# Earlier decoding of packed MLP weights, and earlier loads and splits for the first expert page, in a fused attention, MLP and mixture-of-experts kernel

## The chip, the cores and the metric

The kernel runs on one core of one Trainium2 chip. The metric is device time in microseconds (us) from the program's start to its end: the median of three runs. The five engines of the core that appear below are TensorE (PE; its weight loads are PEld), VectorE (DVE), ScalarE (ACT), GpSimd (POOL) and SyncE (SP), which here only starts transfers. Each engine works through its own list of instructions strictly in order, and waits for the others by semaphores.

## What is computed

```python
def reference(**kwargs):
    # attention: 4 batches, 8 heads, 768 positions, 64 wide;
    # a position sees 4 sink positions and a window of 128
    scores = np.where(is_sink | in_window, scale * q @ k.T, -1e9)
    a = softmax(scores)
    x = (a @ v).transpose(0, 2, 1, 3).reshape(3072, 512)
    # MLP, 512 -> 2048 -> 512
    h = x @ w_in
    x = (h - np.tanh(h)) @ w_out
    # top-1 mixture of 8 experts, 512 -> 1024 -> 512
    e_idx = np.argmax(x @ w_gate + modality_bias[modality_id], axis=1)
    for e in range(8):
        mask = e_idx == e
        out[mask] = gate_w[mask, None] * (np.maximum(x[mask] @ w1[e], 0) @ w2[e])
    return out
```

Everything is float32. The MLP weights arrive in memory as 64-bit words.

## The kernel before

**Precision.** A float32 matrix product is made of three faster products: each operand is split into a high part (a rounding cast, mostly on ScalarE, line 209) and a low part (a subtraction, on GpSimd or VectorE, line 214), and high by high, high by low and low by high are summed.

**The three stages.** The 3072 tokens are handled in 12 chunks of 256. A chunk needs 8 attention units (96 in all; a unit U has scores `s`, line 315 for the first 14 units, a masked row maximum `e`, line 324 on VectorE, an exponential, a normalisation with `sm`, lines 329 to 338, a transposition `T`, lines 348 and 349, and a product with the values `R`, lines 406 to 410). A chunk's MLP then runs over 16 slices f of the hidden width: `L1` (line 176) makes `h` from the chunk's tokens `xt` and the slice `wi`, `gact` (lines 187 to 192) makes `g` from two slices, and `L2` (line 246) adds to `acc` with the slice `wo`. The last stage is the experts: tokens are sorted into pages of 256 rows of one expert each, 13 pages being run always; the page's weights are loaded (`m_wload`, line 745, tile `mr`) and split (`m_wsplit`, ScalarE's cast at line 753, tile `mh`, and VectorE's subtraction at line 754, tile `ml`). The page's list of tokens is loaded by `m_list` (line 762, tile `mpl`) and turned into indices on VectorE (lines 764 and 766, tiles `mi` and `ms`). The order of the first three pages is known after chunk 10 has been routed.

**Decoding.** All 32 half-slices of the MLP weights (`wi0` to `wi15`, `wo0` to `wo15`) are loaded once (`w_load`, line 135, tile `raw`, 512 KB each, issued by SyncE) and decoded once (`w_decode`) out of the 64-bit words, during the first 160 us. A decode is three VectorE instructions (lines 145, 147 and 149), one ScalarE cast and one GpSimd subtraction.

**What sets the order.** Each step is emitted with a due time, and the steps are sorted by it; a scheduler that builds the program then sets the final order within each engine. Sixteen units of due time are one chunk, so one attention unit takes two. The due times come from a table, `self.o`, in line 45: `wl` and `wls` are the first due time and the spacing of the weight loads, `wd` and `wds` those of the decodes, `mwl` and `mws` how far ahead of its use a page's weight slice is loaded and split. `m_events` never lets a step of the first pages be due before the routing is known (`max(t + d, t0)`).

Of the kernel before, what the change touches and what calls it, by code (L numbers as in the profile page):

```python
# [40 lines left out]
class Kern:  # L41
    def __init__(self, tc, a):
        self.tc, self.nc, self.a = tc, tc.nc, a
        self.Wi, self.Wo = {}, {}
        self.o = dict(tc='a', xa='g', mt0=-0.28, gz='v', mxe=11, lx='v', nf=14, efh='a', trc=-14.17, tpf=-1.86, xhi='v', vhi='a', vlo='g', qhi='a', khi='v', sT='a', tr='a', ev='a', glo='g', whi='a', wlo='g', gk=0, wl=-8.54, wls=1.25, wd=-3.86, wds=1.05, wo=1, bs=2, be=3, bE=3, bV=1, bg=2, btr=1, bxt=1, pt={'h': 'h', 's': 'r', 'T': 'r', 'R': 'R', 'x': 'R', 'y': 'R'}, pb=(('r', 2), ('h', 2), ('R', 2)), tl=-9.97, ts=-5.86, tv=-4.34, tsv=-2.34, tS=-5.24, dS=0.07, tN=-4, dN=0.5, tT=-1.78, dT=0.35, tPV=-0.39, txs=-0.28, tg=0.64, tre=0.05, trl=0.48, trr=3.39, u0=-15.64, g=2, lag=3.4, raw=2, sp=2, ghi='a', qlo='g', klo='v', eh='v', xlo='v', x2=4, me=13, mxl=8.77, mxt=1.5, mlag=1.45, mwl=9.99, mws=3.27, mm=0, ev0='v', ghi0='a', vhi0='a', sT0='a', qhi0='a', xlo0='g', eh0='v', y=2)

    def e(self, k, start):
        return self.o.get(k + "0", self.o[k]) if start else self.o[k]
# [786 lines left out]
    def m_events(self, add, g, t, t0=-1e9, ts=(0, 1)):  # L835
        n8 = FF // P
        o = self.o
        at = lambda d, fn, *a: add(max(t + d, t0), fn, *a)
        at(-o["me"], self.m_expert, g)
        x0 = o["mxe"] if g == 1 else o["mxl"]  # L840
        if g < EARLY and t0 > 0:
            add(t0, self.m_list, g)
        else:
            at(-x0 - .01, self.m_list, g)
        at(-x0, self.m_xload, g, ts)
        for j in ts:
            at(-o["mxt"] + 0.5 * j, self.m_xT, g, j, ts)
            at(n8 + o["mlag"] - 0.5, self.m_out, g, j)
        for f in range(n8):
            at(f - o["mwl"], self.m_wload, g, f)  # L850
            at(f - o["mws"], self.m_wsplit, g, f)
            at(f, self.m_L1, g, f, ts)
            at(f + o["mlag"], self.m_L2, g, f, ts)

# [205 lines left out]
```

## Time and profile before

| | us |
|---|---|
| three runs | 1157.36, 1158.56, 1164.47 |
| median | 1158.56 |
| profiled execution | 1158.06 |
| its span, first to last instruction | 1156.3 |
| TensorE busy in the span | 1109.8 |
| VectorE busy in the span | 845.4 |

The three runs show the time of whole executions. The profile is of one execution; the 1.76 us between its time and its span lie around the first and the last instruction. Busy times are of the whole span and are averages over stages that differ: the first 160 us (attention and decoding), the steady chunks, and the pages from about 835 us on.

### The profile page before, as it was taken

How to read it: one execution, taken by the hardware profiler on the slowest of the kernel's cores; microseconds unless marked ns; L12 is line 12 of the kernel's file. 1: busy time of each engine (PE TensorE's matmuls, PEld its weight loads, DVE VectorE, ACT ScalarE, POOL GpSimd, SP SyncE). 2: the span in 40 equal slices, each digit the busy share in tenths (PEclk: the TensorE clock that was granted, in tenths of full speed). 3: DMA queues.
4: the chain of work that ended last, by engine and by line, in shares of the span. 5: the costliest groups of instructions: out<-in, count | busy, mean ns of one | idle time of the engine just before them, and what ended most of it. 6: DMA issues, size and time to landing. Idle time of an engine off the chain costs nothing. (4 is left out here: it accounts for less than half of the span.)

```text
span 1156.3 us, 22180 instructions
## 1 busy us (share of the span) xinstructions
PE 1109.8 (96%) x7143; PEld 978.2 (85%) x7143; DVE 845.4 (73%) x2244; ACT 696.1 (60%) x1669; POOL 586.4 (51%) x847
## 2 busy tenths in 40 slices
PE   7999889999999999999999999999899999999995
PEld 3467678998999999998999998998788989999984
DVE  3389988787888878798888789765687566666640
ACT  3566656666667666667576666664746555555531
POOL 2257775667676767676676767662203211121111
PEclk9999999999999999999999999999999999999998
DMA  6356422223232322222131322100857776677600
GB/s 201 92 188 220 142 71 49 81 74 69 75 70 70 70 78 62 88 65 86 52 94 52 92 65 68 60 10 19 304 188 247 239 231 219 214 233 239 211 21 22
DMA packets 74957, 136.79 MB, mean 118 GB/s; under 512 B 16144, under 2 KB 51216, under 8 KB 74832
## 3 DMA queue, kind: packets, MB, share of 16 engines
q1 hardware_dynamic: 70064, 122.40, 35.0%
q0 software_dynamic: 4768, 12.87, 3.4%
q8 instruction: 59, 0.97, 0.4%
q14 instruction: 66, 0.54, 0.2%
HBM read 122.60 MB, written 12.91 MB: 117 GB/s over the span
## 5 line engine op out<-in xcount | busy, mean ns | idle before, releaser
L176 PE MATMUL h<-xt,wi 128*128 128x256 f32 x2304 | 349.7, 290 | 10.7 <-ACT wi L209 4.3
L176 PEld LDWEIGHTS h<-xt,wi 128*128 128x128 f32 x2304 | 313.5, 193 | 31.1 <-ACT wi L209 6.1
L246 PE MATMUL acc<-wo,g 128*128 128x512 f32 x1152 | 313.9, 399 | 6.0 <-ACT g L209 5.1
L246 PEld LDWEIGHTS acc<-wo,g 128*128 128x128 f32 x1152 | 201.9, 189 | 39.0 <-ACT g L209 5.7
L754 DVE TENSOR_TENSOR ml<-mr,mh 128x1024 fp32r<-128x1024 f32 x104 | 129.3, 1247 | 57.9 <-ACT mh L753 56.7
L214 POOL TENSOR_TENSOR g<-gy,g 128x512 fp32r<-128x512 f32 x96 | 130.9, 1364 | 74.0 <-ACT g L209 70.1
L803 PE MATMUL mh<-mxt,mh 128*128 128x256 f32 (+1 forms) x832 | 154.4, 282 | 1.0 <-ACT mxt L791 0.7
L803 PEld LDWEIGHTS mh<-mxt,mh 128*128 128x128 f32 x832 | 135.7, 191 | 9.5 <-ACT mxt L791 0.9
L820 PE MATMUL macc<-mh,mg 128*128 128x512 f32 x400 | 141.6, 399 | 0.2
L753 ACT CAST mh<-mr 128x1024 fp32r<-128x1024 f32 x104 | 108.9, 1051 | 44.5 <-PE macc L820 29.6
L356 POOL TENSOR_SCALAR_AFFINE_SELECT X<-fl 128x512 fp32r<-128x512 f32 (+1 forms) x192 | 113.2, 612 | 41.8 <-DVE fl L386 23.5
L829 POOL DMA_INDIRECT out_dram<-mo,mi x25 | 26.2, 1046 | 205.7 <-ACT mo L828 202.0
L326 ACT ACTIVATE e<-e,nm 128x160 f32<-128x160 f32 x192 | 81.7, 426 | 79.9 <-DVE nm L324 71.2
L803 PE MATMUL mh<-mxt,ml 128*128 128x256 f32 (+1 forms) x416 | 117.0, 282 | 0.0
L191 ACT ACTIVATE u<-u,kt 128x512 f32<-128x512 f32 x96 | 69.4, 723 | 45.8 <-DVE h L190 30.8
L324 DVE CUSTOM_DVE_ANT_0 e<-s,mask 128x160 f32<-128x160 f32 x192 | 61.3, 319 | 37.0 <-PE T L349 28.4
L214 DVE TENSOR_TENSOR K<-k,K 64x448 fp32r<-64x448 f32 x82 | 85.3, 1040 | 2.7
L214 POOL TENSOR_TENSOR B<-q,A 128x256 fp32r<-128x256 f32 x82 | 70.6, 861 | 31.5 <-ACT A L209 31.2
L820 PEld LDWEIGHTS macc<-mh,mg 128*128 128x128 f32 x400 | 74.4, 189 | 13.3 <-DVE mg L807 1.0
L806 ACT ACTIVATE mg<-mh 128x256 fp32r<-128x256 f32 (+1 forms) x104 | 39.2, 377 | 75.1 <-PE mh L803 70.6
L187 ACT ACTIVATE u<-h 128x512 f32<-128x512 f32 x96 | 56.4, 588 | 40.0 <-PE h L176 39.7
L803 PEld LDWEIGHTS mh<-mxt,ml 128*128 128x128 f32 x416 | 79.3, 191 | 0.0
(230 smaller groups left out, 2196.1 us busy)
## 6 DMA issues: line engine op xcount, KB each, us to landing
mr<-in_moe_w_dram SPq DMA_DIRECT2D x104, 512.0 KB, 4.7
k<-in_k_dram SPq DMA_DIRECT2D x82, 224.0 KB, 2.6
v<-in_v_dram SPq DMA_DIRECT2D x96, 128.0 KB, 2.4
q<-in_q_dram SPq DMA_DIRECT2D x82, 128.0 KB, 2.3
rawi<-in_moe_w_in_dram SPq DMA_DIRECT2D x16, 512.0 KB, 6.2
rawo<-in_moe_w_out_dram SPq DMA_DIRECT2D x16, 512.0 KB, 5.4
x2d<-x SPq DMA_DIRECT2D x24, 256.0 KB, 2.1
k<-in_k_dram SPq DMA_DIRECT2D x14, 112.0 KB, 2.6
```

Of the source, the lines that this page charges most:

```text
L176: nc.tensor.matmul(h, w[:, wl, k * P:(k + 1) * P], x[:, xl, k], start=(n == 0), stop=(n == 11))
L187: nc.scalar.activation(u, h, AF.Square)
L191: nc.scalar.activation(u, u, AF.Relu, bias=self.kt, accum_out=self.over[:, n:n + 1])
L214: (self.nc.vector if eng == "v" else self.nc.gpsimd).tensor_tensor(out=out, in0=a, in1=b, op=ALU.subtract)
L246: nc.tensor.matmul(o, g[:, gl, q:q + P], w[:, wl], start=(f == 0 and n == 0), stop=(f == NF - 1 and n == 2))
L324: nc.vector.tensor_tensor_reduce(out=e, in0=s[:, P:QW], in1=self.mask[min(i, 2)], scale=-0.125, scalar=3.0e38, op0=ALU.add, op1=ALU.min, a ...
L326: nc.scalar.activation(e, e, AF.Exp, bias=nm, scale=-1.0, accum_out=u["sm"][:, t:t + 1])
L356: self.nc.gpsimd.affine_select(out=out, in_=in_, pattern=[[0, n], [s, P]], base=0, channel_multiplier=-s, compare_op=ALU.is_gt if prev els ...
L753: nc.scalar.copy(hi, r)
L754: nc.vector.tensor_sub(lo, r, f32(hi))
L803: nc.tensor.matmul(h, wt[:, k * P:(k + 1) * P], x[:, xl, k, c0:c0 + w], start=(n == 0), stop=(n == 11))
L820: nc.tensor.matmul(self.macc[g][t], gt[:, gl, i * P:(i + 1) * P], w[:, DM:], start=(f == 0 and n == 0), stop=(f == n8 - 1 and n == 2))
```

## The change

Four due times of the MLP weights change, and the first page gets its own two lead times. The loads and decodes begin earlier, and are spaced wider, so that one pair (`wi` and `wo` of one f) falls to about one attention unit; the loads move by nearly the same distance as the decodes. The first page's weights are due 14 f ahead of their use in place of 9.99 to load, and 7 f in place of 3.27 to split.

```diff
-        self.o = dict(... wl=-8.54, wls=1.25, wd=-3.86, wds=1.05, ...
-                      mwl=9.99, mws=3.27, ...)
+        self.o = dict(... wl=-21.0, wls=1.9, wd=-14.0, wds=1.8, ...
+                      mwl=9.99, mwl0=14.0, mws0=7.0, mws=3.27, ...)
...
         for f in range(n8):
-            at(f - o["mwl"], self.m_wload, g, f)
-            at(f - o["mws"], self.m_wsplit, g, f)
+            at(f - (o["mwl0"] if g == 0 else o["mwl"]), self.m_wload, g, f)
+            at(f - (o["mws0"] if g == 0 else o["mws"]), self.m_wsplit, g, f)
```

In the built program the first difference shows on VectorE between the row maxima of the units 4 and 5 (`e4_1` and `e5_1`; `nm` is the maximum, `s` the scores, `ypi` and `ypo` scratch of a decode, `yo` its result). Before:

```order
L317 COPY_PREDICATED s4_1_389<-mgt_74,s4_1_389 128x128
L324 ISA e4_1_393,nm4_1_392<-s4_1_389,mask1_118 128x160
L324 ISA nm4_1_392 128x1
L330 RECIPROCAL sm4_384<-sm4_384 128x2
L324 ISA e5_0_428,nm5_0_427<-s5_0_424,mask0_107 128x160
L324 ISA nm5_0_427 128x1
L317 COPY_PREDICATED s5_1_431<-mgt_74,s5_1_431 128x128
L324 ISA e5_1_435,nm5_1_434<-s5_1_431,mask1_118 128x160
L324 ISA nm5_1_434 128x1
L211 CAST xt0_736<-xp0_1_399 128x256
```

After, from `e5_0` to `e5_1`:

```order
L324 ISA e5_0_482,nm5_0_481<-s5_0_478,mask0_107 128x160
L324 ISA nm5_0_481 128x1
L145 TENSOR_SCALAR ypo2_522<-rawo2_276 128x512
L330 RECIPROCAL sm4_418<-sm4_418 128x2
L317 COPY_PREDICATED s5_1_485<-mgt_74,s5_1_485 128x128
L147 SCALAR_TENSOR_TENSOR ypo2_522<-rawo2_276,ypo2_522 128x512
L149 SCALAR_TENSOR_TENSOR yo2_521<-rawo2_276,ypo2_522 128x512
L145 TENSOR_SCALAR ypi3_558<-rawi3_294 128x512
L147 SCALAR_TENSOR_TENSOR ypi3_558<-rawi3_294,ypi3_558 128x512
L211 CAST xt0_826<-xp0_1_443 128x256
L324 ISA e5_1_489,nm5_1_488<-s5_1_485,mask1_118 128x160
L324 ISA nm5_1_488 128x1
```

Between `e5_0` and `e5_1` stand one whole decode, two instructions of the next, and a cast of the MLP's input; before, only a selection of scores stood there. By the last row maximum of unit 9, 15 of the 32 decodes are through VectorE in place of 3, by the end of chunk 0's first `gact` 17 in place of 5, and by unit 16 31 in place of 27.

TensorE's list around unit 4's scores (`s4`) and unit 2's values product (`R2`). Before:

```order
L315 MATMUL s4_0_382<-k4_234,q4_233 128x288
L315 MATMUL s4_1_389<-k4_234,q4_233 128x288
L406 MATMUL R2_398<-sTn2_376,v2_272 64x256
L407 MATMUL R2_398<-X2_379,v2_272 64x128
L410 MATMUL R2_398<-X2_379,v2_272 64x256
L348 MATMUL T3_411<-ident_69,e3_0_296 128x128
L349 MATMUL T3_411<-ident_69,e3_0_296 128x128
L348 MATMUL T3_411<-ident_69,e3_1_303 128x128
```

After:

```order
L315 MATMUL s4_0_416<-k4_242,q4_241 128x288
L315 MATMUL s4_1_423<-k4_242,q4_241 128x288
L406 MATMUL R2_442<-sTn2_402,v2_284 64x256
L407 MATMUL R2_442<-X2_405,v2_284 64x128
L176 MATMUL h0_0_844<-xt0_826,wi0_383 128x256
L410 MATMUL R2_442<-X2_405,v2_284 64x256
L176 MATMUL h0_0_844<-xt0_826,wi0_383 128x256 x2
L348 MATMUL T3_457<-ident_69,e3_0_310 128x128
L349 MATMUL T3_457<-ident_69,e3_0_310 128x128
L348 MATMUL T3_457<-ident_69,e3_1_317 128x128
```

The first three MLP products stand inside unit 2's values product; ahead of unit 10's first scores (`s10_0`) stand 18 MLP products in place of 9.

At the first page, SyncE's list of transfers, from the first weight slice `mr0_0` on (`mpl1` and `mpl2` are the token lists of the next two pages). Before:

```order
L745 DMA mr0_0_11532<-in_moe2_w_dram 128x1024
L759 TENSOR_LOAD order_344
L759 ISA x2
L762 ISA
L762 DMA mpl1_11543<-xs_63 128x2x2
L759 TENSOR_LOAD order_344
L759 ISA x2
L762 ISA
L762 DMA mpl2_11558<-xs_63 128x2x2
L745 ISA
```

After:

```order
L745 ISA
L745 DMA mr0_1_11534<-in_moe2_w_dram 128x1024
L745 ISA
L745 DMA mr0_2_11536<-in_moe2_w_dram 128x1024
L745 ISA
L745 DMA mr0_3_11538<-in_moe2_w_dram 128x1024
L745 ISA
L745 DMA mr0_4_11540<-in_moe2_w_dram 128x1024
L759 TENSOR_LOAD order_360
L759 ISA x2
L762 ISA
L762 DMA mpl1_11551<-xs_63 128x2x2
```

The slices 1 to 4 now follow the slice 0 directly, and the token lists come behind them.

VectorE's list at the same place, behind the activation step of slices 8 and 9 of chunk 11. Before:

```order
L192 SCALAR_TENSOR_TENSOR gy11_4_11646<-gy11_4_11646,h11_8_11606 128x512
L764 CAST mi0_11528<-mpl0_11526 128x2
L766 SCALAR_TENSOR_TENSOR ms0_11530<-mpl0_11526 128x2
L764 CAST mi1_11545<-mpl1_11543 128x2
L766 SCALAR_TENSOR_TENSOR ms1_11547<-mpl1_11543 128x2
L764 CAST mi2_11560<-mpl2_11558 128x2
L766 SCALAR_TENSOR_TENSOR ms2_11562<-mpl2_11558 128x2
L190 TENSOR_TENSOR h11_10_11657<-u11_5_11705,h11_10_11657 128x512
L192 SCALAR_TENSOR_TENSOR gy11_5_11706<-gy11_5_11706,h11_10_11657 128x512
L754 TENSOR_TENSOR ml0_0_11737<-mr0_0_11532,mh0_0_11736 128x1024
```

After:

```order
L192 SCALAR_TENSOR_TENSOR gy11_4_11658<-gy11_4_11658,h11_8_11614 128x512
L764 CAST mi0_11528<-mpl0_11526 128x2
L766 SCALAR_TENSOR_TENSOR ms0_11530<-mpl0_11526 128x2
L190 TENSOR_TENSOR h11_10_11671<-u11_5_11721,h11_10_11671 128x512
L192 SCALAR_TENSOR_TENSOR gy11_5_11722<-gy11_5_11722,h11_10_11671 128x512
L754 TENSOR_TENSOR ml0_0_11634<-mr0_0_11532,mh0_0_11633 128x1024
L754 TENSOR_TENSOR ml0_1_11668<-mr0_1_11534,mh0_1_11667 128x1024
L754 TENSOR_TENSOR ml0_2_11691<-mr0_2_11536,mh0_2_11690 128x1024
L190 TENSOR_TENSOR h11_12_11735<-u11_6_11780,h11_12_11735 128x512
L764 CAST mi1_11553<-mpl1_11551 128x2
L766 SCALAR_TENSOR_TENSOR ms1_11555<-mpl1_11551 128x2
L764 CAST mi2_11568<-mpl2_11566 128x2
```

The index steps of the pages 1 and 2 (`mi1`, `ms1`, `mi2`, `ms2`) no longer stand ahead of `h11_10`, but behind `h11_12`.

## Rows read from the trace of the kernel before

**Rows 1.** The page: busy time of each engine.
```profile
PE 1109.8 (96%) x7143; PEld 978.2 (85%) x7143; DVE 845.4 (73%) x2244; ACT 696.1 (60%) x1669; POOL 586.4 (51%) x847
```

**Rows 2.** Busy time by stretch: start and end, length, then each engine, clock, DMA.
```profile
core 0: us, PE busy (x) PEld busy (x) DVE busy (x) ACT busy (x) POOL busy (x), PEclk, DMA share, GB/s
24.23:62.75 38.52, 38.03 (x93) 18.34 (x94) 14.17 (x53) 17.50 (x58) 11.04 (x24) 1.00 0.43 130
62.75:152.22 89.47, 77.36 (x401) 58.81 (x401) 86.14 (x185) 59.33 (x150) 67.34 (x81) 0.96 0.53 176
220.00:280.00 60.00, 59.20 (x410) 54.27 (x409) 49.14 (x147) 40.29 (x109) 42.24 (x64) 1.00 0.28 72
```

**Rows 3.** Timeline of TensorE: start, time, engine, line, operation, count, idle before.
```profile
5.66 4.80 PE L315 MATMUL s<-k,q 64*128 64x288 f32 x8 [5.66 <-DMA k<-in_k_dram]
...
24.23 2.39 PE L315 MATMUL s<-k,q 64*128 64x288 f32 x4
47.67 0.42 PE L348 MATMUL T<-ident,e 128*128 128x128 f32 x1
...
62.75 2.28 PE L315 MATMUL s<-k,q 64*128 64x288 f32 x4
64.96 3.57 PE L176 MATMUL h<-xt,wi 128*128 128x256 f32 x15
71.08 1.45 PE L176 MATMUL h<-xt,wi 128*128 128x256 f32 x10 [0.56 <-POOL wi L214]
76.69 0.27 PE L349 MATMUL T<-ident,e 128*128 128x128 f32 x1
...
152.22 0.38 PE L176 MATMUL h<-xt,wi 128*128 128x256 f32 x1 [1.42 <-DVE xt L211]
```

**Rows 4.** VectorE by kind, from 24.23 to 62.75 us.
```profile
L324 DVE CUSTOM_DVE_ANT_0 e<-s,mask 128x160 f32<-128x160 f32 x12 | 3.9, 324 | 15.0 <-PE T L349 14.2 <-PE s L315 0.8
```

**Rows 5.** VectorE's timeline in a run of decodes.
```profile
88.01 0.68 DVE L149 SCALAR_TENSOR_TENSOR yo<-rawo,ypo 128x512 int32<-128x512 int32 x1
88.61 0.69 DVE L147 SCALAR_TENSOR_TENSOR ypi<-rawi,ypi 128x512 int32<-128x512 int32 x1
```

**Rows 6.** VectorE and GpSimd by kind, from 62.75 to 152.22 us.
```profile
L149 DVE SCALAR_TENSOR_TENSOR yo<-rawo,ypo 128x512 int32<-128x512 int32 x15 | 10.2, 680 | 0.1
L214 POOL TENSOR_TENSOR wo<-yo,wo 128x512 fp32r<-128x512 f32 x14 | 18.6, 1328 | 6.0 <-ACT wo L209 6.0
```

**Rows 7.** TensorE's waits from 62.75 to 152.22 us: total, times, longest.
```profile
PE h L176 <- ACT wi L209: 4.3, 6, 1.3
PE h L176 <- POOL wi L214: 2.4, 4, 0.9
```

**Rows 8.** Timeline at the first page: SyncE, VectorE, ScalarE, TensorE.
```profile
813.89 1.77 SPq L762 DMA_DIRECT2D mpl<-xs  x2
815.91 18.20 SPq L745 DMA_DIRECT2D mr<-in_moe_w_dram  x16
...
817.61 0.17 DVE L764 CAST mi<-mpl 128x2 int32<-128x2 f32 x1 [4.05 <-DMA mpl<-xs]
...
819.43 0.72 ACT L191 ACTIVATE u<-u,kt 128x512 f32<-128x512 f32 x1 [3.55 <-DVE h L190]
826.02 1.05 ACT L753 CAST mh<-mr 128x1024 fp32r<-128x1024 f32 x1 [1.12 <-DMA mr<-in_moe_w_dram]
830.18 0.61 ACT L209 CAST g<-gy 128x512 fp32r<-128x512 f32 x1
...
817.89 2.00 PE L246 MATMUL acc<-wo,g 128*128 128x512 f32 x8
830.85 1.40 PE L246 MATMUL acc<-wo,g 128*128 128x512 f32 x4 [3.93 <-ACT g L209]
832.73 3.18 PE L246 MATMUL acc<-wo,g 128*128 128x512 f32 x8 [0.48 <-POOL g L214]
```

**Rows 9.** Busy time by stretch, TensorE waiting for the first page.
```profile
820.00:840.00 20.00, 15.35 (x86) 12.80 (x85) 16.97 (x18) 17.48 (x27) 4.98 (x4) 0.91 1.02 406
```

More of the change, by code (lines that the diff above doesn't have):

```diff
@@ L44, in __init__ @@
         self.Wi, self.Wo = {}, {}
-        self.o = dict(tc='a', xa='g', mt0=-0.28, gz='v', mxe=11, lx='v', nf=14, efh='a', trc=-14.17, tpf=-1.86, xhi='v', vhi='a', vlo='g', qhi='a', khi='v', sT='a', tr='a', ev='a', glo='g', whi='a', wlo='g', gk=0, wl=-8.54, wls=1.25, wd=-3.86, wds=1.05, wo=1, bs=2, be=3, bE=3, bV=1, bg=2, btr=1, bxt=1, pt={'h': 'h', 's': 'r', 'T': 'r', 'R': 'R', 'x': 'R', 'y': 'R'}, pb=(('r', 2), ('h', 2), ('R', 2)), tl=-9.97, ts=-5.86, tv=-4.34, tsv=-2.34, tS=-5.24, dS=0.07, tN=-4, dN=0.5, tT=-1.78, dT=0.35, tPV=-0.39, txs=-0.28, tg=0.64, tre=0.05, trl=0.48, trr=3.39, u0=-15.64, g=2, lag=3.4, raw=2, sp=2, ghi='a', qlo='g', klo='v', eh='v', xlo='v', x2=4, me=13, mxl=8.77, mxt=1.5, mlag=1.45, mwl=9.99, mws=3.27, mm=0, ev0='v', ghi0='a', vhi0='a', sT0='a', qhi0='a', xlo0='g', eh0='v', y=2)
+        self.o = dict(tc='a', xa='g', mt0=-0.28, gz='v', mxe=11, lx='v', nf=14, efh='a', trc=-14.17, tpf=-1.86, xhi='v', vhi='a', vlo='g', qhi='a', khi='v', sT='a', tr='a', ev='a', glo='g', whi='a', wlo='g', gk=0, wl=-21.0, wls=1.9, wd=-14.0, wds=1.8, wo=1, bs=2, be=3, bE=3, bV=1, bg=2, btr=1, bxt=1, pt={'h': 'h', 's': 'r', 'T': 'r', 'R': 'R', 'x': 'R', 'y': 'R'}, pb=(('r', 2), ('h', 2), ('R', 2)), tl=-9.97, ts=-5.86, tv=-4.34, tsv=-2.34, tS=-5.24, dS=0.07, tN=-4, dN=0.5, tT=-1.78, dT=0.35, tPV=-0.39, txs=-0.28, tg=0.64, tre=0.05, trl=0.48, trr=3.39, u0=-15.64, g=2, lag=3.4, raw=2, sp=2, ghi='a', qlo='g', klo='v', eh='v', xlo='v', x2=4, me=13, mxl=8.77, mxt=1.5, mlag=1.45, mwl=9.99, mwl0=14.0, mws0=7.0, mws=3.27, mm=0, ev0='v', ghi0='a', vhi0='a', sT0='a', qhi0='a', xlo0='g', eh0='v', y=2)
     def e(self, k, start):
```

## The prediction

> **What bounds the kernel now.** The page comes first: TensorE is busy for 1109.8 of the 1156.3 us span, VectorE for 845.4 [rows 1]. That is an average over stages, so I read the table of stretches next, and there the reader sees three regimes [rows 2]. From 24.23 to 62.75 us, six attention units, TensorE is busy for 38.03 of 38.52 us while VectorE has only 14.17 us of work. From 62.75 us, unit 10's scores, to 152.22 us, where chunk 1's first MLP product waits 1.42 us for its tokens [rows 3], it is the other way round: VectorE is busy for 86.14 of 89.47 us and TensorE for 77.36. From 220 to 280 us, a steady stretch, TensorE is full again (59.20 of 60) and VectorE has 49.14. So VectorE bounds the second stretch, and the first has room on VectorE. The timeline gives the rate of TensorE: a transposition spends 0.42 us at 47.67 us and 0.27 us at 76.69 us, 15 MLP products take 3.57 us at 64.96 us and 10 take 1.45 us at 71.08 us [rows 3]: 0.238 against 0.145 us each. Up to about 71 us TensorE works at the lower of its two levels, 1.2 GHz, by these durations (the clock column prints 1.00 there, and I go by the durations). The last place is the first page, where TensorE waits 3.93 us for a cast on ScalarE [rows 8].
>
> **Part 1, decoding earlier: the second stretch.** Twelve of the 32 decodes move from behind unit 10's scores to before them. Each is three VectorE instructions of about 0.68 us by the grouped rows [rows 6], but in a run one starts 0.60 us after the other [rows 5]. So 36 instructions, 21.6 to 24.5 us, leave VectorE here, and 61.6 to 64.5 of its 86.14 us stay. GpSimd loses 12 subtractions of 1.33 us [rows 6], 16 us, of its 67.34. TensorE then has: 401 matmuls here [rows 2], less 9 that also move forward, 392, at the steady stretch's 59.20/410 = 0.144 us, 56.4 us; to this the slow beginning, 62.75 to 71.08 us, adds: 25 matmuls ran there, worth 3.6 us at the steady rate, in 8.3 us, so 4.7 us. That is 61 us. Two engines of 61 and 63 us fit less well than one of 86 and one of 60: before, 3.3 us were lost beyond VectorE, and TensorE was idle for 12.1. I take 63 plus those 12, 75 us, since both rely on instructions handed over in order, with two PSUM buffers for the scratch. The gain is 14.5 us. Bounds: 65 us, if it packs as the steady stretch does (gain 24.5), and 81.5 us, if only a third of the removed work shows (gain 8). The named waits of TensorE on decoded weights, 4.3 and 2.4 us [rows 7], are part of it.
>
> **Part 1: the first stretch.** The price stands here. The 9 early MLP products run at 0.238 us, 2.1 us that TensorE, full already, must add. VectorE goes from 14.17 to 36 to 39 us, in a stretch that becomes 41 us long: nearly full as well. Behind the three instructions of a decode waits the row maximum `e`, and behind it ScalarE's exponential, GpSimd's `sm` and the next transposition. Before, VectorE stood idle 15.0 us ahead of 12 row maxima, 14.2 of it for TensorE's transpositions [rows 4], so a decode instruction of 0.7 us mostly falls into a gap of 1.2 us. I add 1.4 us for the times when it doesn't: 3.5 us in all. Bounds: 2 (nothing waits; less than nothing is excluded as long as TensorE stays at its level, since it has no idle time to give back) and 8 (VectorE's 38.7 us and half of the 15.0 stay in sequence: 46.4 in place of 38.5).
>
> The loads cost nothing: one pair now stands ahead of unit 0's values in SyncE's queue. 1 MB at the 406 GB/s seen at the first page [rows 9] is 2.6 us, and the first scores, which wait for their own load until 5.66 us, then take 4.80 us [rows 3], ahead of the first use of those values. Without that cover it would be 2.6 us, once. Behind 152 us the order is the same but for details: 0, within 2 either way.
>
> **Part 2, the first page.** Before, the token lists of pages 1 and 2 were issued by SyncE ahead of the slices 1 to 4, from 813.89 us on for 1.77 us; the next slices followed at 815.91 us. VectorE waited in its list for these token lists, 4.05 us the longest, with the MLP's `h` behind; ScalarE waited 3.55 us for that `h` at 819.43 us [rows 8]. At the end of this chain a cast of `g` started at 830.18 us, and TensorE had idled 3.93 us, then 0.48, and ran 12 products in 4.58 us that at 817.89 us took 0.25 us each, 3.0 us [rows 8]. The change puts slices 1 to 4 first on SyncE and the index steps of the pages 1 and 2 behind two more activation steps on VectorE. ScalarE's 3.55 us go, and the chain moves forward by as much; that nearly empties TensorE's 3.93, and with the gap goes part of the 1.6 us that the lower clock cost. What is late next is ScalarE's own queue, five casts of 1.05 us ahead of that `g`, one of which waited 1.12 us for its load [rows 8]. I take a gain of 4 us. Bounds: 0, if the casts wait for loads as before, and 6, all of 3.93, 0.48 and 1.6. Nothing is behind the moved index steps but splits that have time.
>
> **Sum.** 3.5 - 14.5 - 4 = -15.0 us against the profiled 1158.06 us, of which 1156.3 are span: 1143.1 us. The median of the runs, 1158.56, is 0.5 above that execution, so 1143 us stands for a median too, within 0.5. One per cent, 11.6 us, is about what a measurement of this kernel can tell from no change, so faster means below 1147.0 and slower above 1170.1.
>
> **A page's rule weighed.** The trace counts TensorE busy for 77.36 us in the second stretch, yet 401 matmuls would take 58 us at the steady rate [rows 2]. The Trainium skill, Perfetto Trace Analysis, section Identifying the Most-Contended Engine, says that matmul busy time is no good measure, since pipelined matmuls look longer or shorter in a trace, and that the busy share of weight loads is better. The trace agrees here: weight loads fill 58.81 of 89.47 us, 66%, against 54.27 of 60, 90%, in the steady stretch [rows 2]; at 90% they would need 65 us. By the page's rule the gain is open; taking busy time at its word is the second rival below.
>
> **Rivals.**
> *The page part does not do what it says.* The loads can't be issued before the routing is known, and at 820 to 840 us the DMA engines are full, at 406 GB/s [rows 9]; ScalarE's casts waited for loads there [rows 8]. Against it: the 3.55 us hung on a token list, not on weights. Then 3.5 - 14.5 = -11, 1147 us.
> *Only idle time can be won.* If TensorE's 77.36 busy us in the second stretch are real work, only the 12.1 idle us are to be had, and about half would go: -6 + 3.5 - 4 = -6.5, 1151.5 us. For it: two engines near their limits hand over to each other. Against it: the 0.144 us of the steady stretch.
> *TensorE's clock rises earlier.* In the rows it rises about 6 us after the first dense run of MLP products began, at 64.96 us [rows 3]. If the 9 early ones, from unit 4's scores on, suffice, the first stretch falls to VectorE's 36.5 us, -2 in place of +3.5, and the 4.7 us of slow beginning go: -2 - 14.5 - 4.7 - 4 = -25, 1133 us. Against it: they come two or three at a time between attention products.
> The Trainium skill, TensorE: Matmul & The Clock Gate, section What's actually happening, says that the engine is throttled by default and activity releases it. The trace differs in part: 98% busy with attention [rows 2] did not release it.
> *Slower: the queues hold the row maxima back.* In the first stretch each unit has two row maxima, and up to three decode instructions, 2 us, can stand ahead of each, as between `e5_0` and `e5_1`. If that delay meets TensorE each time, a unit loses 4 us, eight units (3 to 10) 32 us: 32 - 14.5 - 4 = +13.5, 1171.5 us. It decides from 18.5/8 = 2.3 us a unit. For it: TensorE has no other work to put between. Against it: the gaps of 14.2 us in front of the row maxima [rows 4], and scores that run a unit ahead.
>
> **How the numbers follow.** Forecast 0.53, its own range 1134 to 1151; page part without effect 0.13; only idle time 0.20; clock early 0.07; slower 0.07. Below 1147 lie about 0.42 of the forecast's 0.53, 0.06 of the first rival, 0.02 of the second and the 0.07 of the third: 0.57. Above 1170.1 lie 0.05, most of the last. The rest is 0.38. The range: 1131 takes in the early clock; 1153 takes in the idle-time case and stops short of the sum's worst bounds (8 - 8 - 0 = 0, 1158) and of the slower one; what is left out is the 0.07 of that, some 0.04 of the idle-time case and 0.06 of the tails.
>
> **What would show it.** Right: VectorE's decode rows between 24 and 63 us, units there of about 6.6 us in place of 6.04; from unit 10's scores to chunk 1's first product some 75 us; chunk 1 starting near 141 us in place of 152.22; at the first page no VectorE wait on a token list and TensorE's 3.93 us below 1. Wrong: row maxima in the first stretch with long waits behind decodes and TensorE idle on ScalarE's exponential or GpSimd's `sm`; chunk 1's first product at 148 us or later; TensorE waiting as long before the first page, now on casts that wait for `mr`.

## The result, and the profile after

The changed kernel takes 1146.1 us (median of four runs, 1146.07 to 1147.16) against 1158.9 us before (four runs, 1157.36 to 1164.47): a ratio of 0.9882, 95% interval 0.9853 to 0.9910. That is faster by 1.2%, or 12.8 us; 1143 us was forecast. The profiled execution has a span of 1144.4 us in place of 1156.3.

The page's busy times after, to be read beside [rows 1]:

```profile
PE 1105.0 (97%) x7143; PEld 976.7 (85%) x7143; DVE 842.0 (74%) x2244; ACT 696.1 (61%) x1669; POOL 597.5 (52%) x847
```

TensorE's work is the same 7143 products. The stretches that answer to [rows 2], cut at the same instructions (unit 4's scores, unit 10's scores, chunk 1's first MLP product, the middle of chunk 2), and for the last one its partner of the kernel before in a fence of its own:

```profile
core 0: us, PE busy (x) PEld busy (x) DVE busy (x) ACT busy (x) POOL busy (x), PEclk, DMA share, GB/s
24.07:64.52 40.45, 36.88 (x102) 19.07 (x103) 34.90 (x90) 23.43 (x69) 24.80 (x35) 0.78 0.83 234
64.52:138.70 74.18, 70.46 (x382) 54.19 (x383) 58.02 (x135) 47.59 (x126) 47.70 (x62) 0.94 0.41 125
138.70:207.76 69.06, 65.91 (x451) 60.69 (x450) 55.32 (x169) 44.17 (x120) 47.48 (x69) 0.98 0.26 66
```

```profile
152.22:219.39 67.17, 64.40 (x435) 59.32 (x436) 53.90 (x156) 40.31 (x109) 41.65 (x63) 0.97 0.24 67
```

The first stretch is now nearly full on two engines: TensorE is busy for 36.88 of 40.45 us, and VectorE has 34.90 us of work in place of 14.17 in 38.52. The second is 74.18 us long in place of 89.47, and in it VectorE has 58.02 us and TensorE, with 70.46, sets the time. Chunk 1 is longer: 69.06 us and 451 products in place of 67.17 and 435.

TensorE's timeline after, which answers to [rows 3]:

```profile
24.07 2.39 PE L315 MATMUL s<-k,q 64*128 64x288 f32 x4
32.59 2.29 PE L315 MATMUL s<-k,q 64*128 64x288 f32 x4 [1.33 <-DVE nm L324]
39.54 1.30 PE L315 MATMUL s<-k,q 64*128 64x288 f32 x4
44.52 0.75 PE L315 MATMUL s<-k,q 64*128 64x288 f32 x2 [1.05 <-DVE nm L324]
46.12 0.96 PE L315 MATMUL s<-k,q 64*128 64x288 f32 x2 [0.86 <-ACT sTn L209]
50.74 1.32 PE L315 MATMUL s<-k,q 64*128 64x288 f32 x2
64.52 1.33 PE L315 MATMUL s<-k,q 64*128 64x288 f32 x2
...
138.70 0.36 PE L176 MATMUL h<-xt,wi 128*128 128x256 f32 x1
```

The reader sees unit 5's scores wait 1.33 us for the row maximum, units of 8.5 and 7 us at first, a short time at the higher level (four scores in 1.30 us at 39.54 us, not 2.39), two more waits, and the lower level again at 50.74 us. What TensorE waited for in the first stretch, and VectorE for the transpositions, which were 14.2 us in [rows 4]:

```profile
PE s L315 <- DVE nm L324: 2.4, 2, 1.3
PE s L315 <- ACT sTn L209: 0.9, 1, 0.9
```

```profile
DVE e L324 <- PE T L349: 1.3, 2, 0.8
```

Cut at six points, the 12 us come out like this (starts of the instructions named, us):

| stretch | before | after | difference | forecast |
|---|---|---|---|---|
| start to unit 4's scores | 24.23 | 24.07 | -0.2 | 0 |
| to unit 10's scores | 38.52 | 40.45 | +1.9 | +3.5 |
| to chunk 1's first MLP product | 89.47 | 74.18 | -15.3 | -14.5 |
| to the order of the first pages, written | 658.86 | 660.91 | +2.1 | 0 |
| to the first page's first product | 24.67 | 24.24 | -0.4 | -4 |
| to the end of the span | 320.59 | 320.52 | -0.1 | 0 |
| sum | 1156.34 | 1144.37 | -12.0 | -15.0 |

The first page, answering to [rows 8]: transfers, then ScalarE, VectorE, GpSimd and TensorE.

```profile
801.26 3.46 SPq L745 DMA_DIRECT2D mr<-in_moe_w_dram  x5
805.53 1.57 SPq L762 DMA_DIRECT2D mpl<-xs  x2
...
811.03 1.05 ACT L753 CAST mh<-mr 128x1024 fp32r<-128x1024 f32 x1 [2.67 <-DMA mr<-in_moe_w_dram]
817.12 0.62 ACT L209 CAST g<-gy 128x512 fp32r<-128x512 f32 x1
...
814.68 0.17 DVE L764 CAST mi<-mpl 128x2 int32<-128x2 f32 x1 [0.73 <-DMA mpl<-xs]
...
815.18 1.87 POOL L777 DMA_INDIRECT mx<-x2d,ms  x1 [5.70 <-DVE ms L766]
817.36 1.41 POOL L777 DMA_INDIRECT mx<-x2d,ms  x1 [0.30 <-issue]
818.79 1.42 POOL L214 TENSOR_TENSOR g<-gy,g 128x512 fp32r<-128x512 f32 x1
...
817.79 1.95 PE L246 MATMUL acc<-wo,g 128*128 128x512 f32 x4 [1.76 <-ACT g L209]
820.27 3.78 PE L246 MATMUL acc<-wo,g 128*128 128x512 f32 x8 [0.54 <-POOL g L214]
823.85 0.63 PE L803 MATMUL mh<-mxt,mh 128*128 128x256 f32 x2
```

The token lists are issued behind five weight slices now. VectorE's longest wait on them is down from 4.05 us to 0.73, and ScalarE's wait of 3.55 us behind it is gone. But ScalarE waits 2.67 us for a slice instead, two gathers of page 1 (`mx`, at 815.18 and 817.36 us) stand in GpSimd's list ahead of the subtraction of `g` at 818.79 us, and the 12 products behind it take 1.95 and 3.78 us, the time of the lower level.

### The profile page after: what moved, and what is told of

It reads as the page before. It is cut to its first block, busy times and chain, and to the rows that moved or that the text cites. A ratio compares the mean times of both kernels' runs of the same rounds, so it can differ in the third digit from the quotient of the medians.

```text
span 1144.4 us, 22186 instructions
## 1 busy us (share of the span) xinstructions
PE 1105.0 (97%) x7143; PEld 976.7 (85%) x7143; DVE 842.0 (74%) x2244; ACT 696.1 (61%) x1669; POOL 597.5 (52%) x847
## 5 line engine op out<-in xcount | busy, mean ns | idle before, releaser
L214 POOL TENSOR_TENSOR g<-gy,g 128x512 fp32r<-128x512 f32 x96 | 133.2, 1387 | 58.0 <-ACT g L209 52.9
L214 DVE TENSOR_TENSOR K<-k,K 64x448 fp32r<-64x448 f32 x82 | 91.7, 1118 | 2.7
L190 DVE TENSOR_TENSOR h<-u,h 128x512 f32<-128x512 f32 x96 | 65.9, 687 | 18.4 <-ACT u L187 17.5
```

What stands on the lines that cost most here:

```text
L190: nc.vector.tensor_mul(h, u, h)
L214: (self.nc.vector if eng == "v" else self.nc.gpsimd).tensor_tensor(out=out, in0=a, in1=b, op=ALU.subtract)
```

## The experiments

All times are medians; "before" was run again on the same chip, and the ratio is to that.

**One part at a time.**

```diff
 e1_decode_alone
-mwl0=14.0, mws0=7.0
+mwl0=9.99, mws0=3.27
 e2_page_alone
-wl=-21.0, wls=1.9, wd=-14.0, wds=1.8
+wl=-8.54, wls=1.25, wd=-3.86, wds=1.05
```

> The four due times of the MLP weights changed, the first page as before. Theory (the decode part carries the whole gain, the page part 0.4 us): 1146.5 us, some 12 us below before, unit 10's scores to chunk 1's first product 74 us in place of 89.5, and at the first page the 3.93 us idle of TensorE as before. Rival (the page part gave the 4 us that were forecast, and the decode part some 8): 1150 us or more.

> The first page's loads and splits early, the MLP weights as before. Theory (its loads are late and TensorE's lower clock takes the rest back): 1158 us, within 1 us of before; from the order's last cast to the first page's first product 24.2 us in place of 24.7. Rival (the forecast's 4 us are there, and the whole change lost them elsewhere): 1154.5 us.

Measured: the decode part alone 1145.9 us against 1159.0, ratio 0.9877 (0.9851 to 0.9902); the page part alone 1159.6 us, ratio 0.9999 (0.9974 to 1.0023). So the decode part is the whole gain, 13 us, and the page part by itself gives nothing that can be measured.

**Only the loads of the MLP weights early.**

```diff
 e3_loads_alone
-wl=-21.0, wls=1.9, wd=-14.0, wds=1.8, ... mwl0=14.0, mws0=7.0
+wl=-21.0, wls=1.9, wd=-3.86, wds=1.05, ... mwl0=9.99, mws0=3.27
```

> Only the loads of the MLP weights early, the decodes and the first page as before. Theory (the loads cost nothing and win nothing, since decodes waited for VectorE's list and not for data): 1158.5 us, within 1 us of before, unit 4's scores at 24.2 us. Rival (the early loads are what wins, since decodes waited for data): 1150 us or less. Third (they delay the first units' own loads, or hold buffers that are wanted): 1160 us or more.

Measured: 1166.8 us, ratio 1.0068 (1.0043 to 1.0092), 7.8 us slower. The gain does not come from data that arrive sooner. The third reading came true in the sum, but its mechanism does not show as the cause: one product waited 0.99 us for a unit's values, as in the row below, yet unit 4's row maximum stood at 25.45 us, no later than before (25.59), and up to 84 us TensorE had done 217 products in place of 215. All of the loss lies between 84 and 152 us. The wait for one decoded weight was 2.42 us there.

```profile
33.53 1.11 PE L406 MATMUL R<-sTn,v 32*64 32x256 f32 x2 [0.99 <-DMA v<-in_v_dram]
...
130.70 0.50 PE L176 MATMUL h<-xt,wi 128*128 128x256 f32 x2 [2.42 <-ACT wi L209]
```

The two parts of the time up to 152 us, before and then with the loads alone:

```profile
0.00:84.00 84.00, 74.33 (x215) 40.05 (x216) 43.67 (x164) 40.80 (x123) 29.73 (x74) 1.00 0.52 160
84.00:152.00 68.00, 58.66 (x320) 45.50 (x319) 66.88 (x142) 44.62 (x112) 53.68 (x63) 0.95 0.50 167
```

```profile
0.00:84.00 84.00, 73.64 (x217) 39.49 (x218) 42.35 (x163) 40.61 (x123) 30.36 (x75) 1.00 0.70 210
84.00:152.00 68.00, 59.43 (x284) 44.83 (x283) 61.58 (x134) 39.53 (x101) 46.38 (x54) 0.83 0.33 103
```

From 84 to 152 us TensorE was as busy as before (59.43 us against 58.66), but at a mean granted clock of 0.83 in place of 0.95, and it got through 284 products in place of 320. At 58.66/320 = 0.183 us those 36 products are 6.6 us, by this estimate most of the 7.8. So, by this estimate, most of the loss is time at the lower level. Why the level fell for longer, and why the same decodes, due at the same times, hold TensorE up longer there, stays open; the built order differs in other places too, and whether buffers held longer have a part is not shown.

**How far to go.** Half way, and one attention unit further.

```diff
 e4_half_way
-wl=-21.0, wls=1.9, wd=-14.0, wds=1.8
+wl=-14.77, wls=1.575, wd=-8.93, wds=1.425
 e5_decode_earlier
-wl=-21.0, wls=1.9, wd=-14.0, wds=1.8
+wl=-23.0, wls=1.9, wd=-16.0, wds=1.8
```

Both have the first page as before.

> All four due times half way (10 decodes before unit 9's last row maximum, 3 before, 15 after), the first page as before. Theory (VectorE bounds the second stretch up to the point where it and TensorE are even, so the first decodes moved win more than the last): 1150 us, over 8 of the 12 us. Rival (each decode moved wins the same): 7 of 12 moved, 1151.5 us. Third (the price in the first stretch is fixed and not by decode): 1153 us or more.

> Loads and decodes of the MLP weights two units of due time (one attention unit) earlier still than in the change, 17 decodes before unit 9's last row maximum in place of 15; the first page as before. Theory (VectorE is full in the first stretch and TensorE bounds the second, so what leaves the second is paid in the first): 1146 us, within 3 us of the decode part alone. Rival (VectorE still bounds the second stretch): two decodes of 1.8 us less, 1142.5 us.

Measured: half way 1148.5 us, ratio 0.9888 (0.9859 to 0.9918), so 10.5 of 13 us with 7 of 12 decodes; one unit further 1148.1 us against 1157.7, ratio 0.9923 (0.9899 to 0.9947), so some 3 us of the gain lost (the interval just touches that of the decode part alone). The half-way run lies outside the rival's 1151.5 (a ratio of 0.9935), and below even the theory's 1150; the other excludes its rival, 1142.5 (0.9869). So the gain per decode falls, and by the medians it then turns. In the run that goes further TensorE waited for VectorE in the first stretch, as in the changed kernel, and for a load besides:

```profile
32.66 2.29 PE L315 MATMUL s<-k,q 64*128 64x288 f32 x4 [1.23 <-DVE nm L324]
35.87 1.11 PE L406 MATMUL R<-sTn,v 32*64 32x256 f32 x2 [0.93 <-DMA v<-in_v_dram]
```

That these waits are the loss, as the theory had it, is not shown. The order of the first pages is written at 800.54 us with the decode part alone and at 798.91 us one unit further:

```profile
800.54 0.15 DVE L713 CAST order<-oeres 1x3 int32<-1x3 f32 x1
```

```profile
798.91 0.15 DVE L713 CAST order<-oeres 1x3 int32<-1x3 f32 x1
```

So in these profiled executions the further step is 1.6 us ahead at that point, and its span is 1.2 us longer in the end (1145.3 against 1144.1 us): what it lost there, it lost behind the order. The change and the half-way run set an earlier start and a wider spacing together; what the spacing does by itself is not shown.

**The first page.** Four kernels that differ from the changed one by the due times of the first page's splits and of the second page's gathers, and one of the decode part with late gathers.

```diff
 p1_loads_early_splits_late
-mws0=7.0
+mws0=3.27
 p2_gathers_late
-mxe=11
+mxe=4
 p3_gathers_and_splits_late
-mxe=11, ... mws0=7.0
+mxe=4, ... mws0=1.8
 p6_gathers_late_loads_early
-mxe=11, ... mws0=7.0
+mxe=4, ... mws0=3.27
 e6_decode_and_gathers_late
-mxe=11, ... mwl0=14.0, mws0=7.0
+mxe=4, ... mwl0=9.99, mws0=3.27
```

> The change, but the first page's splits due as before (3.27 f ahead), its loads early. Theory (when the slices land sets the casts, and with them the last cast of the MLP's g; the due time of the splits does nothing): from the written order to the first page's first product 24 us, as with the change (24.2), and 1146 us. Rival (the early splits stand in the way of g on ScalarE, and cost what the early loads win): 21 to 22 us, and 1143.5 us.

> The change, but the second page's token gathers on GpSimd due 4 f ahead in place of 11, so that they stand behind the subtraction of the last two g in GpSimd's list. Theory (those gathers, moved ahead of that subtraction by the change, took back 1.2 us): 22.5 to 23 us from the written order to the first page's first product in place of 24.2, and some 1.5 us below the change in all. Rival (GpSimd's place does nothing, the loads set the time): 24.2 us and no difference.

> As the run with late gathers, and the first page's splits due 1.8 f ahead in place of 7. Theory (the landing of the slices sets the casts): the same 22.5 to 23 us. Rival (splits in ScalarE's list hold g): 20 to 21.5 us.

> The change, with the second page's gathers late and the first page's splits due as before. Theory (the landing of the slices, with the gathers out of the way): 20 us from the written order to the first page's first product, 1144 us, like the two runs with late gathers. Rival (each of the two edits adds up: 21.3 and 20.2 in place of 24.2): 17.3 us, 1141 us.

> The decode part alone, and the second page's gathers late, without the page part. Theory (the page part is what frees VectorE's list, and the gathers took it back: both are needed): 23 to 24 us from the written order to the first page's first product, 1146 us. Rival (the gathers alone were what held the page): 20.2 us, 1144 us.

Measured, all from the profiled executions but the last column (us; the cast is ScalarE's of `g` for slices 12 and 13; the complete order is line 713's of all pages; sums can differ by 0.1 from rounding):

| kernel | order to cast | cast to first page product | order to first page product | order to complete order | median |
|---|---|---|---|---|---|
| before | 19.1 | 5.6 | 24.7 | 61.2 | 1158.9 |
| changed | 17.5 | 6.7 | 24.2 | 61.2 | 1146.1 |
| decode alone (e1) | 18.4 | 5.9 | 24.2 | 60.7 | 1145.9 |
| page alone (e2) | 16.9 | 6.7 | 23.6 | 60.4 | 1159.6 |
| splits late (p1) | 16.2 | 5.1 | 21.3 | 58.9 | 1143.9 |
| gathers late (p2) | 16.1 | 4.1 | 20.2 | 59.2 | 1145.3 |
| both, splits at 1.8 (p3) | 15.5 | 4.3 | 19.7 | 58.5 | 1144.6 |
| both, splits at 3.27 (p6) | 16.3 | 4.0 | 20.3 | 60.2 | 1145.1 |
| decode and gathers late (e6) | 18.3 | 5.9 | 24.3 | 61.7 | 1145.3 |

GpSimd's and TensorE's rows at that place, with the gathers late (p2):

```profile
818.16 1.38 POOL L214 TENSOR_TENSOR g<-gy,g 128x512 fp32r<-128x512 f32 x1 [7.34 <-ACT g L209]
...
818.14 1.19 PE L246 MATMUL acc<-wo,g 128*128 128x512 f32 x4 [0.77 <-ACT g L209]
819.59 2.11 PE L246 MATMUL acc<-wo,g 128*128 128x512 f32 x8 [0.26 <-POOL g L214]
821.54 0.28 PE L803 MATMUL mh<-mxt,mh 128*128 128x256 f32 x1
823.01 0.39 PE L803 MATMUL mh<-mxt,mh 128*128 128x256 f32 x1 [1.19 <-DVE mxt L792]
...
825.43 0.47 PE L803 MATMUL mh<-mxt,mh 128*128 128x256 f32 x2 [0.84 <-DVE gy L192]
```

and with the splits late (p1):

```profile
815.65 1.19 PE L246 MATMUL acc<-wo,g 128*128 128x512 f32 x4 [0.56 <-ACT g L209]
818.16 2.11 PE L246 MATMUL acc<-wo,g 128*128 128x512 f32 x8 [1.32 <-POOL g L214]
820.11 0.73 PE L803 MATMUL mh<-mxt,mh 128*128 128x256 f32 x2
...
822.87 0.47 PE L803 MATMUL mh<-mxt,mh 128*128 128x256 f32 x2 [0.84 <-DVE gy L192]
```

With the gathers behind the subtraction, the stretch from cast to page shrinks from 6.7 to 4.1 us. The subtraction starts 0.7 us behind the start of its cast in place of 1.7, and the eight products that need it start 1.45 us behind the first four in place of 2.48: 1.0 us. The other 1.6 us lie in the eight products themselves: TensorE ran all 12 at its higher level, having stood idle for 0.77 us and not 1.76 before them (3.30 us in place of 5.73). The late splits (p1) get a part of it in another way: `g` of slices 10 and 11 no longer stands behind the first split's cast on ScalarE. The two edits don't add up (20.3, not 17.3). Late gathers without the page part (e6) change nothing: 24.3. So at this place the page part is worth 4 us only if the gathers get out of its way, and the gathers' place matters only behind the page part. Of the expectations, p1's theory (24 us) missed and its rival came true; p2 and p3 gained more than any reading had; p6's theory held; e6 came out just above its theory's 24 and far from its rival's 20.2. For p2 the expectation had the gathers' own delay, 1.2 us, and not what the level adds to it. The earlier cast in p1 and p2, 16.2 and 16.1 us in place of 17.5, comes from shorter waits for slices (1.07 us the longest in p2, not 2.67); whether the late gathers cause that is open.

The 3 to 4.5 us at the page's first product overstate the gain: close behind it TensorE waits for VectorE, 0.84 us for `gy` in p1, 1.19 us for `mxt` and 0.84 us for `gy` in p2, waits that the changed kernel does not have there. So 1 to 3 us are left at the complete order, some 37 us later, and the medians, 1143.9 to 1145.3 us, cannot be told from the changed kernel's: their ratios to before are 0.9875 to 0.9888, with intervals that all hold 0.9882.

**Extra products to raise the level.** Each of a unit's two blocks of scores and its transpositions get four more products ahead, 12 in all, whose result the next real product writes over; `self.warm` is the identity.

```diff
 w1_change_and_extra_products, w2_before_and_extra_products
+    def warmup(self, U, t, n):
+        if 1 <= U < 12:
+            for _ in range(n):
+                self.nc.tensor.matmul(t[:, :P], self.warm, self.warm,
+                                      start=True, stop=True)
...
         s = self.ps("s", F32, f"s{U}_{t}")
+        self.warmup(U, s, 4)
...
             u["T"] = self.ps("T", F32, f"T{U}")
+            self.warmup(U, u["T"], 4)
```

> The change, with 12 extra products of 128 columns per unit added on TensorE (units 1 to 11, written over by the next real product, so they compute nothing). Theory (the first stretch is bound by TensorE at its lower level, and dense products raise the level): transpositions at 0.11 us apart from about unit 3 on in place of 0.21, the first stretch falls to VectorE's 35 us, the second loses its slow beginning: 1138 us. Rival (VectorE bounds the first stretch already in the changed kernel): no change within 2 us, though the level rises. Third (the level stays as it is): 1.3 us per unit more, 1156 us.

> The kernel before, with the same 12 extra products per unit. Theory (the price of an early decode is paid only since TensorE is slow and full there; before, VectorE bounds all that follows): units of 3.5 to 4 us in place of 6.04 in the first stretch, but VectorE's 100 us of work from unit 4 to chunk 1 set the end: about 110 us in place of 128, so 1140 us. Rival (units can't go faster, since row maximum, exponential and transposition hand over in turn): 1158 us or more. Third (the level stays): 1170 us.

Measured: 1161.3 us (ten runs, 1157.9 to 1173.6), ratio to before 1.0047 (1.0005 to 1.0089), on top of the change, a loss beyond all three readings; 1188.6 us, ratio 1.0262 (1.0214 to 1.0311), on top of the kernel before. The latter is the third reading, and above it: the level stayed low, with TensorE busy for 54.35 of 54.88 us, and a unit went from 6.04 to 9.20 us (its scores start at 33.22 and at 42.42 us):

```profile
33.22 1.33 PE L324 MATMUL s<-k,q 64*128 64x288 f32 x2
34.48 1.11 PE L310 MATMUL s<-warm 128*128 128x128 f32 x4
35.52 1.33 PE L324 MATMUL s<-k,q 64*128 64x288 f32 x2
42.42 1.33 PE L324 MATMUL s<-k,q 64*128 64x288 f32 x2
...
88.47 0.43 PE L358 MATMUL T<-ident,e 128*128 128x128 f32 x1
```

```profile
24.12:79.00 54.88, 54.35 (x157) 32.59 (x156) 11.94 (x47) 16.40 (x55) 8.73 (x23) 1.00 0.28 86
```

Four extra products took 1.04 us, from 34.48 to the next scores at 35.52, or 0.26 us each, so 12 cost 3.1 us a unit; 1.3 had been expected. Eleven units make 35 us, and the kernel lost 29.5. That shows the first stretch of the kernel before bound by TensorE at its lower level: what is added to it there is paid nearly in full. Whether VectorE would bound the first stretch of the changed kernel if TensorE were fast is not settled: with the change and the extra products the level did rise, at 41.6 us, but the extra products filled TensorE (21.14 of 22 us busy from 42 to 64 us).

## Why the prediction was right, and where it was not

**Second stretch: right in size, by luck in part.** The term was -14.5 and the trace shows -15.3. Its reasoning holds in part: VectorE was relieved and kept 58.0 us (61.6 to 64.5 were said). But the 75 us were put together from VectorE's 63 and TensorE's 12 idle, with TensorE at 61, and in fact TensorE's idle time fell from 12.1 to 3.7 us, and its busy time from 77.4 only to 70.5. So the 75 us came out with another make-up: TensorE, not the hand-over, sets this stretch now, and that both sums are about 75 is luck. The term that was too small is "0.144 us" a product. With the higher level throughout, products here take 0.171 us on average:

```profile
74.33:110.58 36.25, 36.25 (x212) 28.77 (x212) 27.05 (x62) 25.88 (x67) 22.47 (x27) 1.00 0.51 161
```

Among them are those of the units up to 13, of which two of line 315 take 0.75 us at 76.18 us; the steady stretch has none. Busy and idle time both fell, which is why the rival "only idle time can be won" missed. Of the 6.9 busy us that went, a part is 19 products fewer (382 in place of 401). Another part is the level: before, ten MLP products took 2.37 us at 85.48 us and 2.41 us at 114.74 us, the time of the lower level, and the changed kernel has no such spell from 74.33 us to chunk 1. The prediction's estimate of 65 us for the weight loads, worked out beside the Trainium skill, Perfetto Trace Analysis, section Identifying the Most-Contended Engine, pointed the right way, and further than the stretch came: it ended at 74.18 us, with weight loads in 54.19 of them, 73%. The section says of pipelined instructions only that they look smaller; that products can look longer, as the prediction adds, is read from [rows 3], where one MLP product takes 0.38 us at 152.22 us and ten take 1.45 us at 71.08 us.

**First stretch: right in kind.** +3.5 was forecast, +1.9 measured in the profiled execution. That execution had a short time at the higher level. In p2, whose list is the same up to the first page, the same four scores took 2.29 us:

```profile
39.56 2.29 PE L315 MATMUL s<-k,q 64*128 64x288 f32 x4
```

and unit 10's row maximum came at 68.66 us in place of 66.68 us: 2.0 us later, which makes the term about +3.9 where the level stays low. In the changed kernel's execution TensorE waited 2.4 us there for row maxima; the slower rival had the right place, but its waits were 1.33 and 1.05 us at two units, and not 4 us at eight.

**"Behind 152 us ... 0, within 2 either way": just outside.** It was +2.1. At chunk 1's first product the changed kernel was one attention unit less far: unit 18's row maximum came 4.7 us before that product in the kernel before, at 147.53 us, and 7.6 us after it in the changed one, at 146.31. A unit's 16 products at 0.146 us are 2.3 us. A part of the second stretch's gain was work put off.

**First page: the step that failed.** "I take a gain of 4 us" measured 0.4, and by itself the part gave nothing. The step that failed is "Nothing is behind the moved index steps but splits that have time." Behind page 1's index step stand its two gathers on GpSimd, and the change moved them, with it, from ahead of the subtraction of slices 10 and 11 to ahead of that of slices 12 and 13, the one that TensorE waits for. I had counted every instruction on SyncE and VectorE, and not followed the index to GpSimd. ScalarE's 3.55 us did go, but the cast came only 1.6 us sooner, since slices arrived late (a wait of 2.67 us where 1.12 was the longest), and the lower level, counted as a gain of 1.6, cost 1.2 more (5.73 for the 12 products, 4.58 before). The rival "the page part does not do what it says" gave the right size, and the DMA wait is its mechanism, though p1 and p2 show that moving the gathers or the early splits away brings back most of what was missing at this place. At the end of the kernel no run shows a gain from the page part, with the gathers early or late.

**The sum** was 3 us off: +3.6 in this term and +2.1 in the one before, against -0.8 and -1.6 in the two first ones, which hid a part of the miss. The measured 1146 lies 3 us above the forecast, in the forecast's own range. Since the page part gave nothing, the whole gain is that of the first rival's sum, which was put at -11.

**"The loads cost nothing"** held in the change: no wait of TensorE on a load in its first stretch. It is not true of early loads as such: with the loads alone one product waited 0.99 us for a unit's values, and one unit further 0.93 us.

**The signs.** Units of 6.7 us on average in the first stretch (6.6 were said), 74.18 us for the second (75) and chunk 1 at 138.70 us (141) came true. At the first page two did not: VectorE still waited 0.73 us on a token list, and TensorE 1.76 us and not below 1.

**Small slips of the prediction**, none of which moves the sum: six casts and not five stood between the last two casts of `g` before, and 38.7 us and half of 15.0 are 46.2, not 46.4.

## What to carry to other kernels

Where one stretch is bound by one engine and its neighbour by another, moving work across the border pays until both are even: 7 of 12 decodes gave 10.5 us, 12 gave 13, and two more gave nothing further (by the medians some 3 us less). When a step is moved, follow what it produces to every engine that uses it: here a 0.17 us index step carried two gathers with it, into the one gap that mattered. A gain at one place is worth what is left of it further on: 4 us at the page's first product were 1 to 3 us some 37 us later, and none that the medians could show.

## What the runs showed of the hardware

- TensorE's level is not the same from one execution to the next of the same list: at the same instruction, 39.54 and 39.56 us, four scores took 1.30 us in the changed kernel and 2.29 us in p2. In p1's four runs the two with a mean granted clock of 0.977 and 0.982 took 1143.0 and 1143.1 us, the two with 0.994 took 1144.7 us each: the lower mean goes with the faster runs (p2, p3 and p6 show the same; the changed kernel's own four runs do not, with 1146.09 us at 0.980 and 1146.07 us at 0.994). The column reads 1.00 in the first stretch before, where products took the time of the lower level, so the mean seems to count the fall at the end of a short fast time and not the slow time before any change; that is an inference from these rows.
- In w2 TensorE was busy for 54.35 of 54.88 us from 24.12 us on, and a transposition still took 0.43 us at 88.47 us, the time of the lower level. The Trainium skill, TensorE: Matmul & The Clock Gate, section What's actually happening, has activity release the throttle. The measurement differs from the rule taken plainly.
- At the first page, the level was lower for some or all of the 12 products in the five kernels of the table where TensorE had been idle for 1.76 to 3.93 us before them (they took 4.58 to 5.85 us), and higher for all of them in the four where it had been idle for 0.23 to 0.77 us (3.30 to 3.32 us; in p1 with 1.32 us more between the first four and the other eight). That is no rule for other places: in the changed kernel's first stretch the level was low again, at 50.74 us, after waits of 1.05 and 0.86 us.
- A product of 128 columns took 0.26 us at the lower level, and an MLP product of 256 columns of the same type 0.238 us [rows 3]: half the columns were no cheaper.
